# A fused attention, gated-MLP and mixer kernel: half products kept in one accumulator, ScalarE copies between them, sums by accumulating transfers, a new order of all work

## The chip, the core and the metric

The kernel runs on one core of a Trainium2 chip. Its engines each work through their own list of instructions in order: PE (TensorE) multiplies matrices, DVE (VectorE), ACT (ScalarE) and POOL (GpSimd) work element by element, and SP (SyncE) issues most transfers. The metric is device time in microseconds (us); lower is better. Before the change the median of three runs is 398.69 us (397.76 to 398.86).

## The reference: what is computed

Three blocks follow each other, all in float32, on 2 batches of 448 tokens and 768 channels:

```python
# attention, 12 heads of 64
scores = 30 * tanh(q @ k.T / 8 / 30);  attn = exp(scores - max);  x = (attn / sum) @ v
# gated MLP: u, v are the halves of h
h = gelu_tanh(x @ w_in);  v_n = layernorm(v) * g_ln
x = x + (u * (w_sg @ v_n + b_sg)) @ w_out
# mixer: over tokens, then over channels
u = x + (relu(x.T @ w_tok1) @ w_tok2).T
out = u + relu(u @ w_ch1) @ w_ch2
```

## The kernel before, in words

Every product outside attention splits both operands into a high and a low part (fp32r) and multiplies three times, high-high, high-low, low-high. A split is two instructions: `cast` writes the high part on ACT, DVE or POOL, and `rest` subtracts on DVE to get the low part. Weights arrive as 64-bit words; `narrow` turns them into float32 with a scaling of the upper word (line 553 on ACT, 554 on POOL), two ACT passes and DVE passes.

Attention goes over 12 pairs of heads: scores (lines 682, 695), tanh (653) and exp (662) on ACT, values (708, 725), column sums formed on DVE (735, 1290) and summed on PE (757). Its score tiles have two PSUM buffers. While it runs, six rows of `w_in` for v and six for u are narrowed and split, and PE fits in the first products of the gated MLP (line 414).

The last stage, the channel mixer, is two products (`ch1_all`, line 1237 on PE, and `ch2_all`, line 1343) done with seven half-size products each in place of eight (p = 0 to 6) over j = 0 to 5. The sums of operands that this needs are made by DVE additions (`change`, line 1290) or by `gather`, a transfer issued by POOL that adds into its destination (line 1165). The products' sums leave PSUM through `onto`, a DVE addition of a PSUM bank and a tile in SBUF (line 1178). In `ch1_all`, product 0 is copied out by ACT (1266), product 1 is added in the same bank and leaves through a ReLU on ACT (1268), product 2 has a bank of its own, 3 and 4 share one, 5 and 6 share one; five `onto` per j. In `ch2_all` each product runs over all j and three banks before the next.

The order on every engine is set by a planner (`Plan.schedule`). Each operation has a due key, a list of engines that may do it with an estimated duration and a handicap, and the tiles that it reads and writes; the planner simulates the engines and takes the earliest, then the most due. `OFF` shifts keys of single operations, `CH1_ORDER` gives the products' order in `ch1_all`, and `SCALE_ON`, `HI_ON`, `RELU_ON`, `W_ON` say which engines may do what. Tiles come from pools with several buffers (`BUFS`).

Of the kernel before, what the change touches and what calls it, by code (L numbers as in the profile page):

```python
# [32 lines left out]
AHEAD, PACE = (36, 10), 2.2  # L33
# [22 lines left out]
SCALE_ON = {"ch1": {"ACT": 0, "POOL": 200}, "ch2": {"ACT": 0, "POOL": 200}}  # L56
# [30 lines left out]
TURN, STAY = 200.0, 320.8  # L87
TABLE = 1290.0
COLD = 6000.0
EARLY = 74.58  # L90
KQ = 1.69
OFF = {
    "a": {
        (0, 0): 6.9, (0, 1): -3.7, (1, 0): 7.0, (1, 1): 27.0, (1, 2): 12.6, (1, 3): 6.6, (2, 1): 0.7,
        (2, 2): 3.5, (3, 0): 0.7, (3, 2): 8.9, (3, 3): 21.1,
    },
    "d": {
        (8, 0): 1.0,
    },
# [4 lines left out]
    },  # L104
    "f": {
        (0, 0): 1.5, (1, 0): 8.3, (2, 0): 0.4, (3, 0): 1.7, (4, 0): -4.9, (6, 0): -0.7, (7, 0): -0.9,
        (9, 0): -1.6, (10, 0): -7.3, (11, 0): 4.7,
    },
# [4 lines left out]
    },  # L113
# [16 lines left out]
    },  # L130
# [37 lines left out]
class Buf:  # L168


    def __init__(self, tag, shape, dtype):
        self.tag, self.shape, self.dtype = tag, shape, dtype
        self.psum = tag in ("gm", "sc")
        self.ap = None
        self.users = 0
        self.last_writers, self.readers = [], []
        self.end = 0.0
        self.first = None
# [22 lines left out]
class Plan:  # L201
# [40 lines left out]
    def schedule(self):  # L242
# [13 lines left out]
        free = {t: [0.0] * n for t, n in BUFS.items()}  # L256
        for b in {b for o in ops for b in o.bufs if b.tag in free and b.ap is not None}:
            free[b.tag].pop()
# [15 lines left out]
        def earliest(o, way):  # L274
# [7 lines left out]
            for b in o.new:  # L282
                if len(free[b.tag]) <= max(taken[b.tag], queue[b.tag].index(b)):
                    return None
                t = max(t, sorted(free[b.tag])[taken[b.tag]])
                taken[b.tag] += 1
            return t

        while len(order) < len(ops):
# [30 lines left out]
            if o.eng == "PE" and o.mode and t < COLD:  # L320
                dur *= 2
            for w in o.ways:
                ready[w[0]].remove((o, w))
            for b in o.new:
                free[b.tag].sort()
                free[b.tag].pop(0)
# [10 lines left out]
            for b in o.bufs:  # L337
                b.users -= 1
                b.end = max(b.end, o.end + LAT[o.eng])
                if b.users == 0 and b.tag in free:  # L340
                    free[b.tag].append(b.end)
# [9 lines left out]
class Net:  # L351
# [145 lines left out]
    def cast(self, n, out, src, r, w, key=None, on=None, psum=False):  # L497

        nc = self.nc
        made = {  # L500
# [4 lines left out]
                n * 0.84 + 160,  # L505
# [7 lines left out]
    def rest(self, n, out, src, hi, r, w, key=None, on=None, psum=False):  # L513

        nc = self.nc
        args = lambda: dict(out=out(), in0=src(), in1=hi().bitcast(F32), op=ALU.subtract)
# [4 lines left out]
    def split(self, n, hi, lo, src, r, w, key=None, on=None, rest=None, psum=False):  # L521
        self.cast(n, hi, src, r, w, key, on or {"ACT": 0}, psum)
        self.rest(n, lo, src, hi, list(r) + list(w), w, key, rest, psum)
# [1095 lines left out]
```

## Time and profile before

| what | value |
|---|---|
| median of three runs | 398.69 us |
| the profiled execution's own time | 397.94 us |
| its span, first to last instruction | 396.1 us |
| mean granted TensorE clock, share of full speed | 0.997 |
| PE busy | 382.1 us, 96% |
| DVE busy | 328.9 us, 83% |
| ACT busy | 278.9 us, 70% |
| POOL busy | 115.2 us, 29% |

All rows come from one profiled execution, so sums are made against 397.94 us. Of that, 1.84 us lie outside the span. A matmul row's duration includes a pipeline that the next one overlaps, so the pace is read from the distance of starts. Idle time "before" an instruction is followed by what ended it.

### The profile page before, as it was taken

To read this page: it belongs to the slowest core of one execution; us is meant where nothing else is said; L and a number is where in the kernel's file an instruction comes from. 1 tells how busy PE (TensorE), PEld (TensorE's weight loads), DVE (VectorE), ACT (ScalarE), POOL (GpSimd) and SP (SyncE) were. 2 spreads that over 40 slices of the span, in tenths; PEclk is the share of its full clock that TensorE was granted. 3 is DMA by queue.
4 is the path that set the end of the run, shared out by engine and by line. 5 is a ranking of instruction groups with operands and counts; after the bars stand their busy time and mean duration, and the time that the engine had idled before them with its cause. 6 is when DMAs were issued, how large, how long until landed. Compare 5 with 4: busy or idle time off the path is not lost. (4 is left out here: it accounts for less than half of the span.)

```text
span 396.1 us, 6148 instructions
## 1 busy us (share of the span) xinstructions
PE 382.1 (96%) x2048; PEld 293.8 (74%) x2048; DVE 328.9 (83%) x592; ACT 278.9 (70%) x479; POOL 115.2 (29%) x134
## 2 busy tenths in 40 slices
PE   7989999999999999999999999999999999899995
PEld 3222224555578899999999988889999988699984
DVE  1799999988997798947777999997777989987961
ACT  5999999999988678677888787446754472443510
POOL 1001010210022310000043549574431665764200
PEclk9999999999999999999999999999999999999998
DMA  7984445564666638976756998978746795867121
GB/s 241 375 324 126 150 148 171 166 177 129 191 203 205 219 117 273 303 245 181 215 196 166 270 280 175 246 199 199 173 91 173 181 283 113 174 104 123 73 82 68
DMA packets 37772, 74.54 MB, mean 188 GB/s; under 512 B 4449, under 2 KB 25569, under 8 KB 37729
## 3 DMA queue, kind: packets, MB, share of 16 engines
q1 hardware_dynamic: 30240, 63.18, 49.5%
q0 software_dynamic: 7344, 10.75, 16.5%
q8 instruction: 18, 0.29, 0.3%
q14 instruction: 26, 0.20, 0.2%
q10 hardware_dynamic: 144, 0.11, 0.1%
HBM read 50.99 MB, written 12.98 MB: 162 GB/s over the span
## 5 line engine op out<-in xcount | busy, mean ns | idle before, releaser
L1343 PE MATMUL gm<-a,a 128*128 128x448 f32 x252 | 54.9, 366 | 0.0
L1343 PEld LDWEIGHTS gm<-a,a 128*128 128x128 f32 x252 | 47.3, 188 | 3.9
L414 PE MATMUL gm<-a,a 128*128 128x448 f32 (+1 forms) x232 | 46.3, 356 | 0.0
L414 PEld LDWEIGHTS gm<-a,a 128*128 128x128 f32 x232 | 42.0, 188 | 2.1
L662 ACT ACTIVATE a<-a,acap 128x896 f32<-128x896 f32 x42 | 42.7, 1056 | 0.1
L653 ACT ACTIVATE a<-sc,qs 128x896 f32<-128x896 f32 x42 | 41.2, 1017 | 1.3 <-PE sc L682 1.1
L553 ACT ACTIVATE r<-r 128x384 f32<-128x384 f32 (+2 forms) x62 | 36.6, 597 | 3.6 <-DMA r<-ch_in 2.1
L517 DVE TENSOR_TENSOR a<-h,a 128x384 fp32r<-128x384 f32 (+3 forms) x57 | 35.2, 624 | 2.6 <-ACT a L501 1.8
L501 ACT CAST a<-h 128x384 fp32r<-128x384 f32 (+3 forms) x48 | 25.8, 544 | 15.9 <-DMA h<-h 5.7
L1237 PE MATMUL gm<-x,a 128*128 128x448 f32 x162 | 35.9, 369 | 0.6 <-DVE x L517 0.4
L1237 PEld LDWEIGHTS gm<-x,a 128*128 128x128 f32 x162 | 29.9, 188 | 4.7 <-DVE x L517 1.3
L414 PE MATMUL gm<-q,a 128*128 128x448 f32 x160 | 33.2, 366 | 0.0
L1343 PE MATMUL sc<-a,a 128*128 128x448 f32 x126 | 30.5, 371 | 2.1 <-DVE a L517 2.0
L414 PEld LDWEIGHTS gm<-q,a 128*128 128x128 f32 x160 | 30.0, 188 | 2.6
L682 PE MATMUL sc<-q 64*64 64x448 f32 x264 | 30.1, 552 | 1.9 <-ACT a L653 1.7
L708 PE MATMUL gm<-a,v 128*64 128x448 f32 x144 | 31.2, 548 | 0.5 <-ACT a L662 0.2
L414 PE MATMUL gm<-x,a 128*128 128x448 f32 x144 | 30.5, 367 | 0.1
L583 DVE SCALAR_TENSOR_TENSOR t<-r,t 128x384 int32<-128x384 int32 (+2 forms) x40 | 24.3, 610 | 7.4 <-ACT t L575 7.3
L554 POOL TENSOR_SCALAR r<-r 128x384 f32<-128x384 f32 x8 | 11.0, 1380 | 65.9 <-DMA w<-t 60.9
L414 PEld LDWEIGHTS gm<-x,a 128*128 128x128 f32 x144 | 26.8, 188 | 4.4 <-DVE h L788 0.9
L561 ACT ACTIVATE t<-r 128x384 uint16<-128x384 uint16 (+2 forms) x40 | 27.5, 694 | 0.2 <-DVE q L517 0.2
L1343 PEld LDWEIGHTS sc<-a,a 128*128 128x128 f32 x126 | 22.9, 188 | 6.2 <-DVE a L517 4.0
(150 smaller groups left out, 767.2 us busy)
## 6 DMA issues: line engine op xcount, KB each, us to landing
r<-ch_in SPq DMA_DIRECT2D x48, 384.0 KB, 3.8
r<-w_in_in SPq DMA_DIRECT2D x12, 512.0 KB, 5.3
q<-qk_in SPq DMA_DIRECT2D x11, 448.0 KB, 7.0
w<-t SPq DMA_DIRECT2D x24, 192.0 KB, 2.8
v<-va_in SPq DMA_DIRECT2D x12, 256.0 KB, 5.8
r<-w_out_in SPq DMA_DIRECT2D x6, 512.0 KB, 4.9
x<-h SPq DMA_DIRECT2D x12, 224.0 KB, 3.3
h<-x SPq DMA_DIRECT2D x12, 224.0 KB, 4.6
```

The source lines that it names most:

```text
L414: self.nc.tensor.matmul(view(), l, rr, start=(i + m == 0), stop=(i + m == n - 1))
L501: "ACT": ("ACT", n / 1.2 + (60 if psum else 95), lambda: nc.scalar.copy(out(), src()), False),
L517: made = {"DVE": ("DVE", n / 0.96 + 70, lambda: nc.vector.tensor_tensor(**args()), not psum)}
L553: "ACT": ("ACT", n / 1.2 + 130, lambda: nc.scalar.activation(high(), high(), AF.Copy, scale=2.0**-112), False),
L561: lambda: nc.scalar.activation(t.ap.bitcast(U16)[:, 0::2], raw.ap.rearrange("p n t -> p (n t)").bitcast(U16)[:, 1::4], AF.Copy, scale=2.0* ...
L583: lambda: nc.vector.scalar_tensor_tensor(out=t.ap.bitcast(I32), in0=raw[:, :, 1], scalar=3, in1=t.ap.bitcast(I32), op0=ALU.logical_shift_l ...
L653: lambda: nc.scalar.activation(te.ap, sc[:, 0:nn, :S], AF.Tanh, scale=self.qs),
L662: lambda: nc.scalar.activation(te.ap, te.ap, AF.Exp, scale=self.acap),
L682: nc.tensor.matmul(sc[at, h, :S], part(rows, ks), part(rows, QC), start=True, stop=True)
L708: nc.tensor.matmul(A[cols, :S], V[:, 2 * j + h], E[j][:, h], start=(j == 0 and not odd), stop=(j == 2 and odd),)
L1237: nc.tensor.matmul(bank.ap[:, :S], l, r, start=not more and (d, n) == (0, 0), stop=(d, n) == (2, 2), skip_group_check=more)
L1343: nc.tensor.matmul(banks[i].ap[:, :S], l, r, start=not more and (j, n) == (0, 0), stop=(j, n) == (KH - 1, 2), skip_group_check=more,)
```

## The change

Products 0, 2, 5 and 6 (in `ch1_all`) and 0, 2, 4 and 6 (in `ch2_all`) now add up in one accumulator. In `ch1_all` ACT copies the running sum out after each of them (`out_of`); in `ch2_all` ACT does so after 0 and 2 (and after 3, which has the other accumulator), and DVE adds it after 4 and 6. The sign of product 2 is turned in the split of its weights (`sign=-1.0`). The tile c12 is kept negated (`minus_relu`), so that in `ch2_all` the differences of tokens become sums and are made by `gather`. Product 1 in `ch1_all` has a bank of its own. `onto` falls from 45 to 27 instructions, DVE additions of 128x448 (`change`) from 30 to 18, two DVE additions of 128x224 go; ACT copies out of PSUM rise from 9 to 33, ReLUs on ACT of a tile in SBUF from 8 to 14 while the 6 out of a bank go, casts of 128x448 on ACT from 55 to 64. Transfers by `gather` rise from 51 to 63, POOL's casts of weights and tokens (128x384 and 128x448) fall from 40 to 17, its ReLUs from 6 to none. PE's matmuls are the same in number, 756 of them in the two channel products.

Four of the twelve scalings of `w_in` go from ACT to POOL, and POOL's casts of 128x512 rise from one to five. Each tile now has a place in its pool that the planner chose (`slot`); before, only the pool's size was given. The planner's durations for POOL are longer, and all keys in `OFF` are new. The diff, cut:

```diff
-AHEAD, PACE = (36, 10), 2.2
+AHEAD, PACE = (32, 30), 2.2
-SCALE_ON = {"ch1": {"ACT": 0, "POOL": 200}, "ch2": {"ACT": 0, "POOL": 200}}
+SCALE_ON = {"win_v": {"POOL": -200, "ACT": 0}, "win_u": {"POOL": -200, "ACT": 0}, "ch1": {"ACT": 0, "POOL": 200}, "ch2": {"ACT": 0, "POOL": 200}}
+CH1_ORDER += [(2, 0)]
 for j in range(6):
-    CH1_ORDER += [(p, j) for p in ((2, 3, 5, 4, 6) if j < 3 else (0, 2, 3, 1, 5, 4, 6))]
+    CH1_ORDER += [(p, j) for p in (3, 5)] + [(2, j + 1)] * (j < 5) + [(6, j), (4, j)] + [(0, j + 3), (1, j + 3)] * (j < 3)
-    "win_v": ({"DVE": -150}, {"DVE": 0}),
+    "win_v": ({"POOL": -300, "DVE": 0}, {"DVE": 0}),
...
-        (0, 0): 6.9, (0, 1): -3.7, (1, 0): 7.0, (1, 1): 27.0, (1, 2): 12.6, (1, 3): 6.6, (2, 1): 0.7,
+        (0, 0): -1.4, (0, 1): 5.7, (1, 0): 16.8, (1, 1): 29.9, (1, 2): -5.3, (1, 3): 8.0, (2, 0): -0.1,
...
-                    b.ap = pool.tile(b.shape, b.dtype, tag=b.tag, name=f"{b.tag}_{n[b.tag]}", bufs=BUFS[b.tag])
+                    b.ap = pool.tile(b.shape, b.dtype, tag=f"{b.tag}.{b.slot}", name=f"{b.tag}_{n[b.tag]}", bufs=1)
...
+    def out_of(self, out, bank, at):
+        self.act(S, lambda: self.nc.scalar.copy(out.ap, bank.ap[:, :S]), [bank], [out], 60, key=at)
...
             product(0, j, x, a11, o11, False)
-            self.act(S, lambda x=x, o=c12: nc.scalar.copy(o.ap, x.ap[:, :S]), [x], [c12], 60, key=at[0, j])
-            product(1, j, x, a12, o21, True)
-            self.act(S, lambda x=x, o=c11: nc.scalar.activation(o.ap, x.ap[:, :S], AF.Relu), [x], [c11], 60, key=at[1, j])
+            self.out_of(c11, x, at[0, j])
+            product(1, j, w, a12, o21, False)
+            self.onto(c11, w, c11, at[1, j])
+            self.relu(c11, at[1, j])
...
-            product(2, j, y, s2, o2, False)
-            self.onto(c12, y, c12, at[2, j], ALU.subtract)
+            product(2, j, x, s2, o2, True)
+            self.out_of(c21, x, at[2, j])
...
+            product(5, j, x, a21, o1, True)
+            self.out_of(c22, x, at[5, j])
+            self.onto(c22, y, c22, at[5, j])
+            self.relu(c22, at[5, j])
+            product(6, j, x, a12, o22, True)
+            self.out_of(c12, x, at[6, j])
+            self.minus_relu(c12, at[6, j])
+            product(4, j, y, a22, o4, True)
+            self.onto(c21, y, c21, at[4, j])
...
-            self.change(b11[j], b11[j], b12[j], ALU.subtract, S, key(2, j, 16))
-            self.change(t2, b22[j], b11[j], ALU.add, S, key(2, j, 15))
-            product(2, y, j, weight(s2, key(2, j, 9)), tokens(t2, key(2, j, 8)))
+            self.gather(b11[j], b12[j], S, key(2, j, 20) + off("h", 1, j))
+            self.change(t2, b22[j], b11[j], ALU.add, S, key(2, j, 15) + off("h", 2, j))
+            product(2, x, j, weight(s2, key(2, j, 9), -1.0), tokens(t2, key(2, j, 8)), True)
...
-            self.change(b12[j], b22[j], b12[j], ALU.subtract, S, key(3, j, 14))
+            self.gather(b12[j], b22[j], S, key(3, j, 18) + off("h", 3, j))
```

Three places in the lists of instructions follow. The first is ACT at the start of attention: `sc` is a score tile, `a_...<-sc` is tanh, `a<-a,acap` is exp, `r_...` is a raw row of `w_in` being scaled. Before:

```order
L653 ACTIVATE a_189<-sc_165,qs 128x896
L662 ACTIVATE a_189<-a_189,acap 128x896
L553 ACTIVATE r_153<-r_153 128x512
L653 ACTIVATE a_211<-sc_182,qs 128x896
L653 ACTIVATE a_216<-sc_198,qs 128x896
L662 ACTIVATE a_211<-a_211,acap 128x896
L662 ACTIVATE a_216<-a_216,acap 128x896
L653 ACTIVATE a_240<-sc_218,qs 128x896
L653 ACTIVATE a_245<-sc_225,qs 128x896
```

Now:

```order
L680 ACTIVATE a_189<-sc_165,qs 128x896
L689 ACTIVATE a_189<-a_189,acap 128x896
L680 ACTIVATE a_208<-sc_182,qs 128x896
L680 ACTIVATE a_213<-sc_198,qs 128x896
L689 ACTIVATE a_208<-a_208,acap 128x896
L689 ACTIVATE a_213<-a_213,acap 128x896
L680 ACTIVATE a_237<-sc_215,qs 128x896
L680 ACTIVATE a_241<-sc_223,qs 128x896
L689 ACTIVATE a_237<-a_237,acap 128x896
```

The scaling of the raw row between the first exp and the second tanh is gone from ACT, as are two more that came 10 and 13 rows behind it; POOL's first rows behind its memsets are now a scaling, a cast and two more scalings.

The second place is DVE at the head of `ch1_all`: `x_...<-h_...,x_...` is the low part of the operand of product 2, and in the later list `onto` is line 1205, `rest` line 543. Before, the last rows up to it (line 1178 is `onto`, 517 `rest`, 1290 `change`):

```order
L1185 TENSOR_SCALAR h_1730<-h_1730 128x448
L517 TENSOR_TENSOR a_2495<-h_1590,a_2495 128x448
L517 TENSOR_TENSOR a_2519<-v_2210,a_2519 128x384
L517 TENSOR_TENSOR a_2537<-t_2525,a_2537 128x384
L517 TENSOR_TENSOR a_2579<-h_1617,a_2579 128x448
L1290 TENSOR_TENSOR h_1741<-h_1741,h_1590 128x448
L517 TENSOR_TENSOR a_2565<-v_2288,a_2565 128x384
L1290 TENSOR_TENSOR h_1746<-h_1746,h_1610 128x448
L1290 TENSOR_TENSOR h_1806<-h_1806,h_1617 128x448
L517 TENSOR_TENSOR x_2345<-h_1741,x_2345 128x448
```

Now:

```order
L1205 TENSOR_TENSOR q_2518<-q_2518,gm_2534 128x448
L534 SCALAR_TENSOR_TENSOR a_2565<-t_2555,a_2565 128x384
L543 TENSOR_TENSOR a_2371<-v_2182,a_2371 128x384
L1331 TENSOR_TENSOR h_1750<-h_1750,h_1553 128x448
L543 TENSOR_TENSOR a_2572<-a_2276,a_2572 128x384
L543 TENSOR_TENSOR a_2488<-h_1553,a_2488 128x448
L543 TENSOR_TENSOR a_2545<-h_1567,a_2545 128x448
L543 TENSOR_TENSOR a_2510<-h_1557,a_2510 128x448
L1205 TENSOR_TENSOR q_2539<-q_2539,gm_2579 128x448
L610 SCALAR_TENSOR_TENSOR h_2601<-r_2467,h_2601 128x384
L1331 TENSOR_TENSOR h_1785<-h_1785,h_1557 128x448
L543 TENSOR_TENSOR x_2344<-h_1750,x_2344 128x448
```

Counted from the last addition of the token mixer (line 1137 before, 1164 now), the low part of the first operand of product 2 is the 23rd row before and the 22nd now. On PE, product 2 follows the six products (0, j) and (1, j) of j = 0 to 2 at once now; before, product (5, 0) stood between them.

The third place is POOL in `ch2_all`, about where product 1 runs. `TENSOR_SCALAR` is a cast, `DMA` a gather; `x`, `q` and the `a` of a `q<-a` are tokens, all others weights. Before:

```order
L506 TENSOR_SCALAR a_3466<-h_3050 128x384
L1165 DMA v_2707<-a_3392 128x384
L1165 DMA v_2788<-a_3426 128x384
L506 TENSOR_SCALAR a_3511<-x_3206 128x448
L506 TENSOR_SCALAR a_3537<-x_3214 128x448
L1165 DMA a_3392<-a_3392 128x384
L1165 DMA h_2888<-t_3544 128x384
L1165 DMA a_3426<-a_3426 128x384
L1165 DMA v_2824<-a_3501 128x384
L1165 DMA h_3002<-t_3565 128x384
L506 TENSOR_SCALAR a_3616<-v_2601 128x384
L506 TENSOR_SCALAR a_3624<-v_2668 128x384
```

Now:

```order
L1192 DMA v_2587<-h_2846 128x384
L1192 DMA q_2518<-q_2518 128x448
L1192 DMA v_2700<-h_2967 128x384
L1192 DMA q_2539<-q_2539 128x448
L1192 DMA v_2734<-h_3039 128x384
L1192 DMA q_2720<-q_2720 128x448
L1192 DMA q_2584<-q_2584 128x448
L1192 DMA q_2920<-q_2920 128x448
L1192 DMA q_2518<-a_2672 128x448
L1192 DMA v_2741<-h_3129 128x384
L1192 DMA v_2814<-h_3182 128x384
L1192 DMA v_3020<-h_3219 128x384
```

The casts have left the list, and transfers that add tokens to tokens (`q<-q`, `q<-a`) have come in.

## Rows read from the trace of the kernel before

**Rows 1.** Windows: stretch, length, busy (xinstructions) of PE, PEld, DVE, ACT, POOL; clock, DMA.
```profile
0.00:62.00 62.00, 55.32 (x390) 17.23 (x392) 49.49 (x81) 56.36 (x65) 3.94 (x12) 1.00 0.67 231
110.00:232.00 122.00, 122.00 (x625) 110.21 (x624) 99.48 (x183) 95.62 (x185) 23.76 (x29) 1.00 0.71 220
232.00:256.00 24.00, 23.26 (x111) 20.18 (x110) 23.52 (x48) 16.28 (x35) 18.23 (x16) 1.00 0.95 222
312.00:348.00 36.00, 33.89 (x162) 29.46 (x162) 34.28 (x64) 15.87 (x32) 23.73 (x23) 1.00 0.84 189
```

**Rows 2.** PE's list in attention: start, duration, instruction, [idle before <-releaser].
```profile
10.29 0.59 PE L695 MATMUL sc<-a,a 64*64 64x448 f32 x2 [1.77 <-ACT a L653]
...
16.98 0.97 PE L757 MATMUL gm<-a,ones 128*64 128x448 f32 x4 [0.23 <-DVE a L1290]
...
26.04 1.51 PE L682 MATMUL sc<-q 64*64 64x448 f32 x12 [1.75 <-ACT a L653]
...
40.45 0.97 PE L757 MATMUL gm<-a,ones 128*64 128x448 f32 x4 [0.48 <-DVE a L1290]
```

**Rows 3.** ACT's list at the start of attention.
```profile
8.68 0.65 ACT L553 ACTIVATE r<-r 128x512 f32<-128x512 f32 x1 [1.20 <-DMA r<-w_in_in]
9.24 1.89 ACT L653 ACTIVATE a<-sc,qs 128x896 f32<-128x896 f32 x2
...
17.42 0.68 ACT L553 ACTIVATE r<-r 128x512 f32<-128x512 f32 x1
```

**Rows 4.** DVE's list, at the start and at the head of ch1_all.
```profile
9.83 1.42 DVE L605 SCALAR_TENSOR_TENSOR t<-r,t 128x512 int32<-128x512 int32 x2
...
12.35 1.15 DVE L735 SCALAR_TENSOR_TENSOR a<-a,guard,a 128x896 f32<-128x896 f32 x1
...
233.67 0.61 DVE L1137 TENSOR_TENSOR h<-gm,h 128x448 f32<-128x448 f32 x1
...
245.17 0.62 DVE L517 TENSOR_TENSOR x<-h,x 128x448 fp32r<-128x448 f32 x1
```

**Rows 5.** POOL's lines (ns min/median/max): scaling, casts, gathers; how long transfers land.
```profile
L554 POOL TENSOR_SCALAR r<-r x8: 1232/1290/1675, 200.9 to 280.8; 128x384 f32<-128x384 f32 x8
L506 POOL TENSOR_SCALAR a<-v x11: 502/531/5355, 208.8 to 344.9; 128x384 fp32r<-128x384 f32 x11
L1165 POOL DMA_DIRECT2D h<-h x10: 869/917/2647, 245.2 to 294.3; - x10
DMA to landing us min/median/max: 3.0/4.7/12.1
```

**Rows 6.** PE's list at the head of ch1_all, and a piece without a wait.
```profile
245.07 0.36 PE L1237 MATMUL gm<-x,a 128*128 128x448 f32 x1
245.85 4.10 PE L1237 MATMUL gm<-x,a 128*128 128x448 f32 x17 [0.41 <-DVE x L517]
249.79 1.99 PE L1237 MATMUL gm<-a,a 128*128 128x448 f32 x9
...
312.47 1.99 PE L1237 MATMUL gm<-x,a 128*128 128x448 f32 x9
314.30 2.60 PE L1343 MATMUL gm<-a,a 128*128 128x448 f32 x12
```

**Rows 7.** PE's list in ch2_all.
```profile
337.86 0.97 PE L1343 MATMUL sc<-a,a 128*128 128x448 f32 x4
339.42 0.67 PE L1343 MATMUL sc<-a,a 128*128 128x448 f32 x2 [0.60 <-DVE a L517]
...
344.19 1.33 PE L1343 MATMUL sc<-a,a 128*128 128x448 f32 x4
346.43 0.67 PE L1343 MATMUL sc<-a,a 128*128 128x448 f32 x2 [0.92 <-DVE a L517]
```

**Rows 8.** DVE's list in ch2_all, an addition behind a ReLU of POOL.
```profile
325.15 0.62 DVE L1290 TENSOR_TENSOR q<-q 128x448 f32<-128x448 f32 x1 [1.22 <-POOL q L1194]
```

**Rows 9.** Groups by line: busy us, mean ns of one, idle before.
```profile
L1266 ACT COPY q<-gm 128x448 f32<-128x448 f32 x6 | 3.2, 528 | 1.0 <-PE gm L1237 1.0
```

More of the change, by code (lines that the diff above doesn't have):

```diff
@@ L255, in schedule @@
             queue[tag] = [e[2] for e in q]
-        free = {t: [0.0] * n for t, n in BUFS.items()}
+        free = {t: [(0.0, i) for i in range(n)] for t, n in BUFS.items()}
         for b in {b for o in ops for b in o.bufs if b.tag in free and b.ap is not None}:
-            free[b.tag].pop()
+            free[b.tag].remove((0.0, b.slot))
         ready = defaultdict(list)
@@ L321, in schedule @@
                 dur *= 2
+            if o.eng == "DVE":
+                dur += 18.0
             for w in o.ways:
@@ L495, in consts, with cast @@
         self.plan.op([("PE", 800 + 480 * WARM, spin, False, 0)], -30.0, [], [warm])
-    def cast(self, n, out, src, r, w, key=None, on=None, psum=False):
+    def cast(self, n, out, src, r, w, key=None, on=None, psum=False, sign=1.0):
         nc = self.nc
+        if sign < 0:
+            turn = lambda e: e.tensor_scalar(out(), src(), -1.0, None, ALU.mult)
+            made = {
+                "ACT": ("ACT", n / 1.2 + 95, lambda: nc.scalar.activation(out(), src(), AF.Copy, scale=-1.0), False),
+                "DVE": ("DVE", n / 1.92 + 70, lambda: turn(nc.vector), True),
+                "POOL": ("POOL", n * 2.5 + 190, lambda: turn(nc.gpsimd), False),
+            }
+            ways = [made[e] + (t,) for e, t in on.items()]
+            return self.plan.op(ways, self.key - 8 if key is None else key, r, w)
         made = {
@@ L511, in cast, with rest @@
         return self.plan.op(ways, self.key - 8 if key is None else key, r, w)
-    def rest(self, n, out, src, hi, r, w, key=None, on=None, psum=False):
+    def rest(self, n, out, src, hi, r, w, key=None, on=None, psum=False, sign=1.0):
         nc = self.nc
+        if sign < 0:
+            return self.dve(
+                n,
+                lambda: nc.vector.scalar_tensor_tensor(
+                    out=out(), in0=src(), scalar=-1.0, in1=hi().bitcast(F32), op0=ALU.mult, op1=ALU.subtract
+                ),
+                r,
+                w,
+                key=key,
+                port=True,
+            )
         args = lambda: dict(out=out(), in0=src(), in1=hi().bitcast(F32), op=ALU.subtract)
@@ L519, in rest, with split @@
         return self.plan.op(ways, self.key - 8 if key is None else key, r, w)
-    def split(self, n, hi, lo, src, r, w, key=None, on=None, rest=None, psum=False):
-        self.cast(n, hi, src, r, w, key, on or {"ACT": 0}, psum)
-        self.rest(n, lo, src, hi, list(r) + list(w), w, key, rest, psum)
+    def split(self, n, hi, lo, src, r, w, key=None, on=None, rest=None, psum=False, sign=1.0):
+        self.cast(n, hi, src, r, w, key, on or {"ACT": 0}, psum, sign)
+        self.rest(n, lo, src, hi, list(r) + list(w), w, key, rest, psum, sign)
     def weight(self, src, n, key, name, after=None):
@@ L1164, in gather @@
         self.plan.op(
-            [("POOL", 1000.0, lambda: nc.gpsimd.dma_start(out=out.ap, in_=a.ap, accum_op=ALU.add), False, 0)],
+            [("POOL", 1150.0, lambda: nc.gpsimd.dma_start(out=out.ap, in_=a.ap, accum_op=ALU.add), False, 0)],
             at,
@@ L1303, in ch2_all @@
         whole = [self.buf("x", [128, 4, S]) for _ in range(KH)]
-        pairs = [self.a([128, 2, 384]) for _ in range(KH)]
+        pairs = [self.a([128, 2, 384]) for _ in range(KH // 2)]
         rows = lambda i: [Part(x, lambda ap: ap[:, i]) for x in whole]
@@ L1307, in ch2_all @@
         a12 = [self.h([128, 384]) for _ in range(KH)]
[L1308 removed]
+        a21 = [self.h([128, 384]) for _ in range(KH)]
+        a22 = [Part(pairs[j // 2], lambda ap, j=j: ap[:, j % 2]) for j in range(KH)]
         part, spare = rows(0), rows(3)
@@ L1373, in ch2_all @@
         for i in three:
-            t = part[i]
-            self.act(S, lambda i=i, t=t: nc.scalar.copy(t.ap, x[i].ap[:, :S]), [x[i]], [t], 60, key=key(1, 0, 4))
+            self.out_of(part[i], x[i], key(1, 0, 4))
+            self.gather(U[0][i], part[i], S, key(1, 0))
         for j in js:
-            product(1, x, j, weight(a12[j], key(1, j, 9)), tokens(b21[j], key(1, j, 8)), True)
+            product(1, w, j, weight(a12[j], key(1, j, 9)), tokens(b21[j], key(1, j, 8)))
         for i in three:
-            z = U[0][i]
-            self.onto(z, x[i], z, key(2, 0))
-            store(z, i, 0, key(2, 1))
-        y = banks()
+            u = U[0][i]
+            self.onto(u, w[i], u, key(2, 0))
+            store(u, i, 0, key(2, 1))
         for j in js:
@@ L1394, in ch2_all @@
+            self.gather(b12[j], b22[j], S, key(3, j, 18) + off("h", 3, j))
+            self.gather(a21[j], a22[j], 384, key(4, j, 20))
         for i in three:
-            self.onto(part[i], y[i], part[i], key(3, 0), ALU.subtract)
-        z = banks()
+            self.out_of(part[3 + i], x[i], key(3, 0, 4))
+            self.gather(U[0][3 + i], part[3 + i], S, key(3, 0))
+        y = banks()
         for j in js:
-            product(3, z, j, weight(a11[j], key(3, j, 9)), tokens(b12[j], key(3, j, 8)))
+            product(3, y, j, weight(a11[j], key(3, j, 9)), tokens(b12[j], key(3, j, 8)))
@@ L1399, in ch2_all @@
         for i in three:
-            self.onto(part[3 + i], z[i], part[i], key(4, 0, 4))
-            u = U[0][3 + i]
-            self.gather(u, part[i], S, key(4, 0))
+            self.out_of(part[i], y[i], key(4, 0, 4))
+            self.gather(U[1][3 + i], part[i], S, key(4, 0))
         for j in js:
-            product(4, z, j, weight(a22[j], key(4, j, 9)), tokens(b21[j], key(4, j, 8)), True)
+            product(4, x, j, weight(a21[j], key(4, j, 9)), tokens(b11[j], key(4, j, 8)), True)
+        for i in three:
+            u = U[1][3 + i]
+            self.onto(u, x[i], u, key(5, 0, 4))
+            store(u, 3 + i, 1, key(5, 1))
@@ L1405, in ch2_all @@
+        for j in js:
+            product(5, y, j, weight(a22[j], key(5, j, 9)), tokens(b21[j], key(5, j, 8)), True)
         for i in three:
             u = U[0][3 + i]
-            self.onto(u, z[i], u, key(5, 0))
-            store(u, 3 + i, 0, key(5, 1))
-            u = U[1][3 + i]
-            self.gather(u, part[3 + i], S, key(5, 0))
-            u = U[1][i]
-            if i < 2:
-                self.gather(u, part[i], S, key(5, 1))
-                continue
-            for n, o in enumerate(self.last_out):
-                cs = slice(n * S // 2, (n + 1) * S // 2)
-                self.combine(
-                    S // 2,
-                    lambda o=o: o.ap,
-                    lambda u=u, cs=cs: u[:, cs],
-                    lambda i=i, cs=cs: part[i].ap[:, cs],
-                    ALU.add,
-                    [u, part[i]],
-                    [o],
-                    key(5, 3),
-                )
@@ L1427, in ch2_all @@
-        v = banks(self.last_bank)
-        for j in js:
-            product(5, v, j, weight(a21[j], key(5, j, 9)), tokens(b11[j], key(5, j, 8)))
-        for i in three:
-            u = U[1][3 + i]
-            last = self.onto(u, v[i], u, key(6, 0, 4))
-            store(u, 3 + i, 1, key(6, 0))
+            last = self.onto(u, y[i], u, key(6, 0, 4))
+            store(u, 3 + i, 0, key(6, 0))
         if not self.anycap:
@@ L1437, in ch2_all @@
         for j in js:
-            product(6, v, j, weight(a12[j], key(6, j, 9)), tokens(b22[j], key(6, j, 8)), True)
+            product(6, x, j, weight(a12[j], key(6, j, 9)), tokens(b22[j], key(6, j, 8)), True)
         for i in range(2):
             u = U[1][i]
-            self.onto(u, v[i], u, key(6, 5))
+            self.onto(u, x[i], u, key(6, 5))
             store(u, i, 1, key(6, 5))
```

114 lines of the change are left out of this document (59 added, 55 removed), and 53 rows, old and new, of the table OFF.

## The prediction

> **What bounds the kernel now.** I read the windows first, then the waits of PE, then the lists of the engines that PE waited for. In the windows the reader is to see that PE is the bound nearly everywhere: from 110 to 232 us it is busy in 122.00 of 122.00 us [rows 1]. The change leaves PE's matmuls as they are in number, so a gain can come only out of the time in which PE stands. That time is small and lies in three places: attention (55.32 us busy of the first 62), the head of `ch1_all` (23.26 of 24) and a stretch of `ch2_all` (33.89 of 36). In the last two DVE is as full as PE, 23.52 of 24 and 34.28 of 36; in attention it is ACT that is full, 56.36 of 62 with its start-up in it.
>
> PE's list in attention shows whom it waited for: 1.77 us at 10.29 and 1.75 us at 26.04 for a tanh on ACT, which has to free one of two score tiles, and 0.23 and 0.48 us for DVE's sums [rows 2]. ACT's list tells why: between its first exp and its second tanh it stood 1.20 us until a raw row of `w_in` had landed and then scaled it, 9.24 - 8.68 = 0.56 us; together 1.76 us, PE's first wait. Two more such scalings follow within 3 us, the first at 17.42 [rows 3].
>
> In the channel mixer I measure PE's loss by its pace: nine matmuls without a wait take 314.30 - 312.47 = 1.83 us, 0.203 each. At the head of `ch1_all` one matmul takes 245.85 - 245.07 = 0.78 us, a loss of 0.58, and the next 17 take 3.94 us, a loss of 0.48; 1.06 together [rows 6]. In `ch2_all` four matmuls take 1.56 and 2.24 us where 0.81 would do: 0.75 and 1.43 lost [rows 7], and a third such place before them I take at 0.7, about the smaller of the two; 2.9 us together.
>
> **The change, part by part.** *Attention.* Four of twelve scalings and a few casts leave ACT and DVE for POOL, which is busy 3.94 us of the first 62 [rows 1]. At the start ACT goes from its first exp straight to the next tanh: 1.76 us earlier. Not all of it stays. The first row's conversion on DVE now waits for POOL, and DVE does its work in order, so the first column sums stand behind it. POOL's scaling of 384 elements takes at least 1.23 us [rows 5], so 512 take an estimated 1.64: ready at 8.68 + 1.64 = 10.3 in place of 9.24. Behind it DVE has three conversions (two took 1.42, a third an estimated 0.4), three additions of about 1.15 each and one low part (about 0.6) [rows 4]: 10.3 + 1.8 + 3.5 + 0.6 = 16.2. PE's first sum was at 16.98 [rows 2] and can now be at about 16.3: 0.7 us gained there. ACT keeps the rest as a lead over PE, and without the two further scalings it should not be waited for at 26.04; I count that 1.75 us as gone. Of the waits for DVE's sums I count nothing. Term: -2.5 us. Bounds: -4.2 (the four waits of rows 2 all gone) and +1.5 (POOL late, below).
>
> *110 to 232 us.* PE has no idle time there, so the new order can only add; DVE's 99.48 of 122 us leaves room. I take +0.3, bounds 0 and +1.5.
>
> *Head of `ch1_all`.* PE first needs the six products (0, j) and (1, j), 54 x 0.203 = 11.0 us, and then product 2. Before, product 5 stood between, nine matmuls or 1.83 us of cover. DVE's way to the first operand of product 2 is hardly shorter: 22 rows behind the token mixer's last addition where it was 23, and these took 245.17 - 233.67 = 11.5 us [rows 4], so 0.5 each. Two `onto` of product 1, which DVE did not have to do before, are among them. DVE gets there 0.5 us sooner and PE 1.83 us sooner: the first wait grows from 0.58 to about 1.9, and most of the second (0.48) goes, as PE comes later. Term: 1.9 - 1.06 = +0.8 us. Bounds: -1.06 (no wait) and +2.5.
>
> *Rest of `ch1_all`.* Two `onto` fewer per j on DVE, two copies more on ACT of 0.528 us [rows 9]. The copy stands on PE's path: product 6 may add to the accumulator only when product 5 has been copied out. One product stands between, 1.83 us; copy and an ACT instruction in progress (0.65, rows 3) take 1.18. Hidden, so 0; if ACT is one more instruction behind, it costs nothing still, two more 0.65 for each of six j, +3.9.
>
> *`ch2_all`.* Twelve additions of tokens and six `onto` leave DVE, at about 0.6 us (the like row: 0.61) [rows 4], plus two halves: some 11 us of the 34.28 busy in 36 [rows 1] and what follows. POOL loses its ReLUs and nearly all casts there; DVE stood 1.22 us behind one such ReLU [rows 8]. ACT takes six more copies, 3.2 us, beside 15.87 us busy in 36. DVE is then ahead of PE by several us where it was behind, and I count 2.5 of the 2.9 us as gone. Bounds: -2.9 and +4 (the transfers, below). The new transfers replace additions that DVE did itself. From the last use of the tokens to the addition that needs their sum there are 20 rows on DVE, 10 us at 0.5; issue and landing take 0.92 + 4.7 us in the median [rows 5]. Hidden, so 0.
>
> Tile places: they decide which earlier reader a write waits for; the trace does not price them apart, and they are in the bounds.
>
> Sum: -2.5 + 0.3 + 0.8 - 2.5 = -3.9 us, on 397.94 us: 394.0. The median of the runs is 0.75 above the profiled execution; I add half of it: 394.4 us.
>
> At one place a rule speaks against this. POOL's cast of 384 elements took 0.53 us in the median and 5.36 at most [rows 5]. The Trainium skill (SBUF — State Buffer, Who interferes with whom) says that a DVE instruction with two SBUF inputs contends with a GpSimd instruction that reads SBUF. The trace agrees in that the factor of ten is there. By that rule the nine scalings and casts that now run on POOL in attention, beside DVE's additions, would be long ones, and attention's term would be nearer its bound of +1.5 than -2.5; I hold to -2.5, because in the first 20 us DVE waits for POOL rather than working beside it. What the rule would make of the whole is the second rival.
>
> **The rivals.** *The head of `ch1_all` grows (396.8 us).* PE's wait for product 2 becomes 3.5 us, its bound of +2.5, and copies by ACT cost another 0.7: for it, DVE is full there (23.52 of 24); against it, DVE has a row less. 394.4 + (2.5 - 0.8) + 0.7 = 396.8.
>
> *POOL's work in attention takes its gain back (398.2 us, no change).* Each of the nine operations has DVE work behind it. If three of them are as long as 5.36 us and DVE stands 1.22 us behind each, as in rows 8, that is 3.7 us: 394.4 + 3.7 = 398.1. For it: the longest cast; against it: POOL is idle 58 of 62 us, so most are done early.
>
> *Transfers of tokens land late (401 us, slower).* In `ch2_all` DVE's addition for product 2 waits for its gather and everything behind waits too. It decides from a landing of 10 - 0.9 = 9.1 us on. Landing reached 12.1 and an issue on POOL 2.65 [rows 5]: 3.0 + 1.7 = 4.7 us late. One such wait, and one of 3 us behind it, is 7.7 us, less 1 us of lead that I leave to DVE: 394.4 + 6.7 = 401.1. For it: twelve more transfers on one queue; against it: the median of 4.7.
>
> **How the numbers follow.** Forecast 0.60, with its own range of 391.5 to 396.5; head of `ch1_all` 0.15; no change 0.14; slower 0.11. A measurement of this kernel tells 0.3% from no change, 397.5 to 399.9 us around 398.69. The first two cases are faster, 0.75 and a little of the third, 0.01; same 0.13; slower 0.11. The range of 8 in 10 goes from 391.0, a little inside the sum of the good bounds (398.3 - 4.2 - 1.06 - 2.9 = 390.1), to 398.2, which takes in the no-change case and leaves out the late transfers.
>
> **What would show it.** Right: no ACT scaling between the first exp and the second tanh, PE's fifth group of matmuls at about 8.5 us in place of 10.29, no wait above 0.5 us for a tanh after 20 us; one wait of 1 to 2.5 us for `x` on DVE at the first product 2; no PE wait for DVE in `ch2_all`, where DVE should show idle time, and POOL nothing but gathers. Wrong: PE waiting for ACT's copy in `ch1_all` at each j; DVE waiting for DMA in front of the additions of `ch2_all`; a PE wait anywhere between 110 and 232 us; a DVE wait for POOL's casts in attention of more than a microsecond.

## The result, and the profile after

The changed kernel takes 393.61 us (median of four runs, 393.18 to 394.10) against 398.31 of the kernel before: a ratio of 0.9882, 95% interval 0.986 to 0.9905. The forecast was 394.4. The profiled execution took 394.1 us with a span of 391.9, the slowest of the four.

The total came out, but not by the forecast's terms: attention fell 2.2 us short of its term and the channel mixer went 2.4 us past its own. That the two cancel is luck. I set three marks on TensorE's list in both traces: the first 128x128 matmul behind the last sums of attention, the first matmul of `ch1_all`, and the modelled end of the last one of `ch2_all`.

| stretch | before, us | after, us | difference | forecast |
|---|---|---|---|---|
| start to end of attention | 115.44 | 115.12 | -0.3 | -2.5 |
| on to the head of `ch1_all` | 116.53 | 116.73 | +0.2 | +0.3 |
| channel mixer, 756 matmuls | 159.84 | 155.74 | -4.1 | -1.7 |
| rest of the profiled execution's own time | 6.13 | 6.51 | +0.4 | 0 |

The windows that answer to [rows 1], in the same columns:

```profile
0.00:62.00 62.00, 56.49 (x400) 18.35 (x400) 50.00 (x82) 56.56 (x63) 16.09 (x20) 1.00 0.67 232
110.00:232.00 122.00, 121.77 (x621) 109.65 (x620) 99.48 (x184) 99.83 (x197) 12.69 (x18) 1.00 0.68 211
232.00:256.00 24.00, 22.37 (x109) 19.75 (x108) 23.82 (x46) 18.64 (x39) 12.91 (x16) 1.00 1.11 266
312.00:348.00 36.00, 36.00 (x180) 33.39 (x179) 33.41 (x66) 18.67 (x40) 25.40 (x30) 1.00 1.14 197
```

The last row shows the gain: TensorE has no idle time from 312 to 348 us, 180 matmuls where there were 162. In `ch2_all` its list names no wait at all, where [rows 7] had 0.60 and 0.92 us.

In attention it is otherwise. TensorE's list, answering to [rows 2]:

```profile
8.67 0.97 PE L722 MATMUL sc<-a,a 64*64 64x448 f32 x4
10.80 0.59 PE L722 MATMUL sc<-q 64*64 64x448 f32 x2 [1.16 <-DMA q<-qk_in]
...
17.64 0.97 PE L784 MATMUL gm<-a,ones 128*64 128x448 f32 x4 [1.05 <-DVE a L1331]
...
24.72 1.88 PE L709 MATMUL sc<-q 64*64 64x448 f32 x16 [0.38 <-ACT a L680]
...
43.07 0.97 PE L784 MATMUL gm<-a,ones 128*64 128x448 f32 x4 [0.49 <-DVE a L1331]
```

The two waits of 1.77 and 1.75 us for a tanh are gone: the fifth group starts at 8.67 instead of 10.29, and at 24.72 only 0.38 us is left. But directly behind the fifth group TensorE now waits 1.16 us for the second pair's keys, and at the first sums 1.05 us for VectorE. GpSimd's list, then VectorE's, say why the sums are late:

```profile
9.46 1.57 POOL L581 TENSOR_SCALAR r<-r 128x512 f32<-128x512 f32 x1 [7.55 <-DMA r<-w_in_in]
13.02 1.46 POOL L521 TENSOR_SCALAR a<-t 128x512 fp32r<-128x512 f32 x1 [2.00 <-DVE t L632]
14.63 2.24 POOL L581 TENSOR_SCALAR r<-r 128x512 f32<-128x512 f32 x1
```

```profile
11.06 0.43 DVE L621 TENSOR_SCALAR t<-r 128x512 int32<-128x512 int32 x1 [6.04 <-POOL r L581]
11.52 1.42 DVE L632 SCALAR_TENSOR_TENSOR t<-r,t 128x512 int32<-128x512 int32 x2
12.86 1.15 DVE L762 SCALAR_TENSOR_TENSOR a<-a,guard,a 128x896 f32<-128x896 f32 x1
14.11 1.31 DVE L1331 TENSOR_TENSOR a<-a,a 128x896 f32<-128x896 f32 x1
15.34 1.15 DVE L543 TENSOR_TENSOR a<-t,a 128x512 fp32r<-128x512 f32 x1
16.42 1.07 DVE L1331 TENSOR_TENSOR a<-a,a 64x896 f32<-64x896 f32 x1
```

VectorE stands until GpSimd has scaled the raw row at 11.03, then does three conversions of `w_in`, and only then the three additions that the first sums wait for (L762 and twice L1331).

At the head of `ch1_all` there is one wait of the size forecast, at another tile. TensorE's list, answering to [rows 6]:

```profile
242.67 6.95 PE L1277 MATMUL gm<-x,a 128*128 128x448 f32 x33 [1.51 <-DVE q L1205]
```

It stands not at product 2 for operand `x` but one product sooner, at product 1 of the third j, which needs the accumulator that VectorE's addition (242.00 to 242.61) has yet to read.

### The profile page after: what moved, and what is told of

Read it like the earlier page. It is cut to its first block, busy times and chain, and to the rows that moved or that the text cites. A ratio compares the mean times of both kernels' runs of the same rounds, so it can differ in the third digit from the quotient of the medians.

```text
span 391.9 us, 6112 instructions
## 1 busy us (share of the span) xinstructions
PE 380.2 (97%) x2048; PEld 295.6 (75%) x2048; DVE 312.9 (80%) x571; ACT 298.1 (76%) x523; POOL 94.5 (24%) x116
## 5 line engine op out<-in xcount | busy, mean ns | idle before, releaser
L543 DVE TENSOR_TENSOR a<-h,a 128x384 fp32r<-128x384 f32 (+3 forms) x63 | 36.8, 587 | 5.5 <-ACT a L516 4.9
L516 ACT CAST a<-h 128x384 fp32r<-128x384 f32 (+3 forms) x56 | 29.9, 537 | 14.3 <-DVE h L1071 4.8
L580 ACT ACTIVATE r<-r 128x384 f32<-128x384 f32 (+2 forms) x66 | 38.4, 584 | 2.0 <-DMA r<-ch_in 1.7
L709 PE MATMUL sc<-q 64*64 64x448 f32 x264 | 31.0, 552 | 1.0 <-ACT a L680 0.9
L735 PE MATMUL gm<-a,v 128*64 128x448 f32 x144 | 30.4, 548 | 0.1
L1390 PE MATMUL sc<-a,a 128*128 128x448 f32 x126 | 28.7, 364 | 0.0
L602 ACT ACTIVATE t<-r 128x384 f16<-128x384 f32 (+2 forms) x40 | 27.8, 694 | 0.0
L1331 DVE TENSOR_TENSOR a<-a,a 128x896 f32<-128x896 f32 (+1 forms) x24 | 26.6, 1108 | 0.4
```

Source lines behind the costliest of these rows:

```text
L516: "ACT": ("ACT", n / 1.2 + (60 if psum else 95), lambda: nc.scalar.copy(out(), src()), False),
L543: made = {"DVE": ("DVE", n / 0.96 + 70, lambda: nc.vector.tensor_tensor(**args()), not psum)}
L580: "ACT": ("ACT", n / 1.2 + 130, lambda: nc.scalar.activation(high(), high(), AF.Copy, scale=2.0**-112), False),
L602: lambda: nc.scalar.activation(t.ap.bitcast(F16)[:, 1::2], raw[:, :, 1].bitcast(F32), AF.Copy, scale=sign),
L709: nc.tensor.matmul(sc[at, h, :S], part(rows, ks), part(rows, QC), start=True, stop=True)
L735: nc.tensor.matmul(A[cols, :S], V[:, 2 * j + h], E[j][:, h], start=(j == 0 and not odd), stop=(j == 2 and odd),)
```

## The experiments

Two theories of the channel mixer's 4 us: A, VectorE was the bound there and was relieved; B, tiles' planned places took waits for earlier readers away. For attention: ScalarE's freed time was gained and lost again at VectorE and at a transfer; or it never bound. All medians are against 398.28 to 398.78 of the kernel before on the same chips.

**1 and 2. Tile places.** The changed kernel with pools in rotation, and the kernel before with planned places; every engine's order stays.

```
- tag=f"{b.tag}.{b.slot}", ..., bufs=1
+ tag=b.tag, ..., bufs=BUFS[b.tag]
```

> The changed kernel with one thing undone: a tile takes the next place of its pool in turn, as before the change, and not the place that the planner freed. No engine's order changes. Theory A (the 3.9 us that the channel mixer gained come from relief of VectorE: additions into transfers, sums copied out by ScalarE): 393.2 to 394.6 us, no wait of TensorE beyond those of the changed kernel. Theory B (planned places took waits for a tile's last reader away, and that is the gain): 396 to 398.5 us, with waits of TensorE or VectorE in the second channel product that the changed kernel doesn't have.

> The kernel before with one part of the change: tiles get the place that the planner freed. No engine's order changes. Theory A (relief of VectorE is the gain): 397.3 to 398.7 us, with the three waits of TensorE for VectorE in the second channel product (331, 339 and 346 us; 2.0 us together) still there. Theory B (places are the gain): 394.5 to 396.5 us and those waits gone or below 0.8 us together.

Measured: 394.45 us (0.9897, 0.9879 to 0.9915) and 398.29 us (0.999, 0.9969 to 1.0011). Planned places alone give nothing. The list of waits of TensorE in that run (engine, tile, line; total, times, longest) has the three waits of `ch2_all` in full, in its second row:

```profile
PE sc L683 <- ACT a L654: 2.1, 2, 1.7
PE sc L1344 <- DVE a L518: 2.0, 3, 0.9
PE sc L696 <- ACT a L654: 1.6, 1, 1.6
```

With the planned places undone in the changed kernel the median is 0.8 us higher, which the two intervals don't separate; its trace has one wait more, at the head of `ch1_all`, for a copy by ScalarE:

```profile
253.28 0.87 PE L1277 MATMUL gm<-a,a 128*128 128x448 f32 x3 [1.26 <-ACT a L1228]
```

Theory B fails as the source of the gain.

**3. Twelve token additions back on VectorE.**

The two `gather` calls for b11 and b12 (cut) become, at the same places of the order:

```
+ nc.vector.tensor_tensor(out=out.ap, in0=out.ap, in1=a.ap, op=ALU.add)
```

> The changed kernel with the twelve additions of token tiles in the second channel product (b11 and b12, 128x448) on VectorE instead of in transfers, at the same places in the order. VectorE gets 12 x 0.535 us = 6.4 us more; it is 33.41 of 36.00 us busy from 312 to 348 us. Theory A: the slack of 2.6 us there is used up, waits of TensorE for VectorE come back, 395 to 397.5 us. Theory B (places): 393.2 to 394.3 us, no such wait. A third possibility, that VectorE's additions are ready earlier than a transfer (0.6 us against some 5 us), so that nothing is lost: 393 to 394 us.

Measured: 396.17 us (0.9941, 0.992 to 0.9963), 2.6 above the changed kernel, as theory A says. TensorE's list in `ch2_all`, then windows of that run:

```profile
338.17 0.36 PE L1401 MATMUL sc<-a,a 128*128 128x448 f32 x1
340.07 0.68 PE L1401 MATMUL sc<-a,a 128*128 128x448 f32 x2 [1.54 <-DVE a L543]
341.17 1.09 PE L1401 MATMUL sc<-a,a 128*128 128x448 f32 x3 [0.43 <-ACT a L509]
342.08 2.43 PE L1401 MATMUL gm<-a,a 128*128 128x448 f32 x6
344.31 1.93 PE L1401 MATMUL sc<-a,a 128*128 128x448 f32 x6
346.08 3.80 PE L1401 MATMUL gm<-a,a 128*128 128x448 f32 x18
```

```profile
337.00:340.00 3.00, 1.53 (x8) 1.09 (x6) 3.00 (x7) 0.00 (x0) 0.00 (x0) 1.00 0.66 201
340.00:342.00 2.00, 1.50 (x5) 0.83 (x6) 2.00 (x6) 0.98 (x2) 1.22 (x2) 1.00 0.25 94
342.00:344.00 2.00, 2.00 (x7) 1.77 (x7) 1.80 (x5) 0.93 (x2) 1.52 (x3) 0.52 0.93 149
344.00:346.00 2.00, 2.00 (x8) 1.79 (x7) 1.97 (x5) 0.93 (x2) 1.35 (x2) 0.63 0.96 151
346.00:348.00 2.00, 2.00 (x12) 1.85 (x11) 0.79 (x2) 0.46 (x1) 0.28 (x1) 1.00 1.02 167
```

VectorE is busy without a gap from 337 to 342 us while TensorE waits for it. The clock column of these windows belongs to the last section; the profiled execution is the slowest of six (398.13 us), and with 397.83 one of two that stand apart: the other four took 395.63 to 396.44. So the additions cost these four 2.0 to 2.8 us against the changed kernel's median.

**4. The four scalings back on ScalarE.** `nc.gpsimd.tensor_scalar(high(), ...)` becomes `nc.scalar.activation(high(), ..., scale=2.0**-112)`, places unchanged.

> The changed kernel with the four w_in scalings (128x512) that it has on GpSimd during attention issued by ScalarE at the same places of the order. Theory A (the freed ScalarE time was worth some 2 us, and the changed kernel lost it again at the wait for the second pair's keys, 1.16 us, at the first sums, 1.05 us, and by more changes of TensorE's tile shapes, 0.6 us): giving the time back to ScalarE costs 1 to 3 us, 394.6 to 396.6 us; the end of attention moves from 115.12 to 116 or later. Rival (ScalarE's time doesn't bind in attention, the matmuls do): 393.2 to 394.2 us and the end at 115.1 to 115.5.

Measured: 395.16 us (0.9917, 0.9899 to 0.9934), 1.5 above the changed kernel; attention ends at 116.43 us. Both long waits for a tanh are back in TensorE's list:

```profile
10.20 0.59 PE L722 MATMUL sc<-a,a 64*64 64x448 f32 x2 [1.89 <-ACT a L680]
...
25.94 1.50 PE L709 MATMUL sc<-q 64*64 64x448 f32 x12 [1.91 <-ACT a L680]
```

So these scalings caused the two waits, and in this order their removal is worth 1.5 us, not the 3.8 us that the waits measure.

**5 and 6. What took the rest: the sums' place, or the keys?** VectorE's list is changed by setting the start by which an operation is sorted:

```
+ MOVED = {334: 13300.0, 335: 13400.0, 336: 13500.0, 337: 13600.0, 338: 14200.0}   # w_in behind the sums' additions
+ (second run) 332: 2110.0                                     # the first w_in load behind the second pair's keys
```

> The changed kernel with VectorE's first three w_in operations (tile t, behind GpSimd's scaling at 9.46 us) moved behind the second addition of the first pair's sums, and its fourth behind the third addition; nothing else moves. In the changed kernel the sums' additions stand behind them and TensorE waits 1.05 us at 17.64 us. Theory A (that order is what took the gain of attention): first sums at 16.4 to 16.9 us, and 0.6 to 1.1 us of it is still there at the end of attention (115.12 us before): 392.5 to 393.2 us. Rival (ScalarE, busy almost throughout from 11 us, sets the pace whatever the sums do): sums earlier, but the end of attention at 114.9 to 115.3 and 393.3 to 394.0 us.

> As the run with the sums' additions first, and in addition the load of the second pair's keys and queries is issued ahead of the first w_in load (512 KB) instead of behind it. Theory A: the wait of 1.16 us at 10.80 us goes, TensorE's fifth group starts at 9.6 to 10.0 us, ScalarE follows a whole us earlier, the end of attention at 113.0 to 113.8 and 391.3 to 392.3 us. Rival (what comes early is given back, since w_in's rows come later or ScalarE paces): 392.8 to 394 us.

Measured: 392.66 us (0.9851, 0.9822 to 0.9881) and 392.54 us (0.9847, 0.9817 to 0.9878). The sums' order gives 0.95 us, the theory's figure. VectorE's list of the first run:

```profile
10.57 1.15 DVE L769 SCALAR_TENSOR_TENSOR a<-a,guard,a 128x896 f32<-128x896 f32 x1 [5.46 <-ACT a L696]
11.83 1.09 DVE L1338 TENSOR_TENSOR a<-a,a 128x896 f32<-128x896 f32 x1
12.84 0.43 DVE L628 TENSOR_SCALAR t<-r 128x512 int32<-128x512 int32 x1
13.30 1.45 DVE L639 SCALAR_TENSOR_TENSOR t<-r,t 128x512 int32<-128x512 int32 x2
14.67 1.08 DVE L1338 TENSOR_TENSOR a<-a,a 64x896 f32<-64x896 f32 x1
```

Two additions are done before the conversions start, TensorE's first sums come at 15.89 in place of 17.64, and attention ends at 113.83. The other profiles with the sums first and the loads in their old order (runs 11 and 12) end it at 113.77 and 114.54, where six without it had 114.8 in the mean. The load's order adds nothing that the medians show: in the second run the keys land at 7.39 us in place of 9.69 and the raw row of `w_in` at 9.22 in place of 8.32, and the median moves by 0.12 us, less than theory A asked for. The first of the two runs has no wait for keys either, with SP's order unchanged. Executions with the same order up to there waited 0 to 1.27 us for these keys (last section), so the 1.16 us of the profile above is no fixed price.

**7 and 8. The head of `ch1_all`.**

In words, both runs give product (1, 2) its accumulator in place "sc.1", idle until 249 us. The second run also puts VectorE's four rows for `x` and their two additions ahead of `onto(1, 1)`, and ScalarE's copy of `x` (its cast to the high part) ahead of a ReLU.

> The changed kernel with one accumulator moved: product 1 of the third j (its sixth product) gets a bank of a pair that stands idle until 249 us, and so doesn't wait at 242.67 us (1.51 us) for VectorE's addition at 242.00. No order changes. Theory A (behind that wait stands the one forecast, for the low part of operand x at 243.54 to 244.15 us): TensorE waits some 1.2 us one product later, gain 0.2 to 0.5 us, 393.1 to 393.5 us. Rival (the bank was the only wait): gain 1.2 to 1.5 us, 392.1 to 392.4 us.

> As the run with the accumulator moved, and VectorE makes the parts of operand x (tiles x, h) ahead of the addition at 242.00 us and of the merge of raw weights behind it; ScalarE's ReLU of the sum moves behind its copy of x. Theory A: both waits at the head go but for some 0.5 us, gain 0.8 to 1.4 us against the changed kernel, 392.2 to 392.8 us. Rival (given back at the next products, 251.88 and 253.50 us, since VectorE has no idle time up to 256 us): 393.2 to 394.0 us.

Measured: 393.31 us (0.9867, 0.9837 to 0.9897) and 394.33 us (0.9894, 0.9863 to 0.9925). With its own bank product (1, 2) starts at once, and TensorE waits for the operand that the forecast named:

```profile
240.67 1.98 PE L1280 MATMUL aside<-x,a 128*128 128x448 f32 x9
242.49 0.37 PE L1280 MATMUL gm<-x,a 128*128 128x448 f32 x1
243.66 5.09 PE L1280 MATMUL gm<-x,a 128*128 128x448 f32 x23 [0.81 <-DVE x L546]
```

By pace (a stretch's length less 0.2033 us for each matmul in it) the head up to 265 us loses 2.1 us, against 2.3 in the changed kernel and 2.1 in runs 3, 5 and 10 with the old bank: the wait only moved. The second run is slower than both of its theories. In it ScalarE stood 2.63 us at the copy of `x` that I had moved forward, until VectorE had made `h`; all that ScalarE had behind it came later, and TensorE then waited for ScalarE three times (0.75, 0.17, 0.63 us):

```profile
244.05 0.57 ACT L526 CAST x<-h 128x448 fp32r<-128x448 f32 x1 [2.63 <-DVE h L1343]
```

**9. The kernel before, with its first four scalings on GpSimd and nothing else moved.**

> The kernel before with one part of the change: the first four w_in scalings (128x512) are issued by GpSimd at the places where ScalarE had them; nothing else moves. The forecast's term for attention was -2.5 us for taking them off ScalarE: by it the end of attention comes at 113.0 us and the run at 395.6 to 396.2. Theory A (the relief is worth the 1.5 us that the run with the scalings back on ScalarE showed, and VectorE's additions for the sums then stand behind GpSimd's scaling, which takes 1.6 us and more against 0.65): end of attention at 114 to 115 us, TensorE's first sums with a wait of 0.5 to 1.5 us, 396.6 to 397.6 us. Rival (the order of the changed kernel is needed for any gain): 398.0 to 398.6 us.

Measured: 399.74 us (1.0018, 0.9999 to 1.0036) against 398.78: no gain, where the forecast's term by itself would have given 2.5 us. Attention ends at 116.58. GpSimd's and VectorE's rows around the last of the four:

```profile
23.87 1.15 DVE L741 SCALAR_TENSOR_TENSOR a<-a,guard,a 128x896 f32<-128x896 f32 x1
24.12 4.61 POOL L558 TENSOR_SCALAR r<-r 128x512 f32<-128x512 f32 x1 [6.81 <-DVE t L600]
24.93 0.69 DVE L611 SCALAR_TENSOR_TENSOR t<-r,t 128x512 int32<-128x512 int32 x1
25.53 1.09 DVE L1296 TENSOR_TENSOR a<-a,a 128x896 f32<-128x896 f32 x1
26.53 0.70 DVE L611 SCALAR_TENSOR_TENSOR t<-r,t 128x512 int32<-128x512 int32 x1
27.27 1.45 DVE L1296 TENSOR_TENSOR a<-a,a 64x896 f32<-64x896 f32 x1
```

The same operation took 1.58 us at 8.59, while VectorE stood. TensorE's waits for VectorE's sums grow to 1.80 us at 17.49 and 1.11 at 39.91. The first wait for a tanh is gone; the second is still 1.32 us, at 25.83. My expectation (396.6 to 397.6) was too good; nearest is the rival, that the relief needs the new order, and the median lies 1.1 us above its range too. The profiled execution is the fastest of twelve (397.65 us), so these rows show where attention's gain went, not what made the median 1 us worse.

**10. Six copies of `ch2_all` on VectorE.** `nc.scalar.copy` becomes `nc.vector.tensor_copy` behind products 2 and 3.

> The changed kernel with the six copies out of accumulators behind products 2 and 3 of the second channel product on VectorE instead of ScalarE, at the same places of the order. VectorE gets 6 x 0.535 = 3.2 us more. Theory A (the token additions in transfers carry the gain of the second channel product; at the places of the copies VectorE has room, 25.08 of 39.59 us busy from 348 us, and the banks are not wanted at once): 393.2 to 394.2 us, no wait of TensorE. Rival (the copies on ScalarE are as needed as the transfers): 394.6 to 396 us with waits of TensorE for VectorE in the second channel product.

Measured: 394.02 us (0.9883, 0.986 to 0.9906); the channel mixer takes 155.54 us, with no wait in `ch2_all`. These copies carry nothing of the gain.

**11 and 12. Gains together.** The sums first and the bank; then also VectorE's rows for `x` early, with ScalarE's order left alone.

> The changed kernel with the sums' additions ahead of the first w_in operations on VectorE and the sixth product's own accumulator, both as in their runs. If the two gains (0.95 and 0.3 us) add: 392.1 to 392.6 us, faster than either kernel; if the wait for operand x takes the second back: 392.5 to 393.0 us.

> As the run with the sums first and the sixth product's own accumulator, and on VectorE the parts of operand x come directly behind the addition of product 1 of the second j, with the two merges of raw weights behind them; ScalarE's order stays as it is (in the run that moved its copy of x too, ScalarE stood 2.63 us). Theory A: TensorE's wait of 0.81 us for x falls to some 0.5 us or less, nothing waits for ScalarE that didn't before, 391.6 to 392.3 us. Rival (VectorE has no idle time here, so the merges come later and the wait only moves to the next weights): 392.3 to 393.3 us.

Measured: 392.67 us (0.9844, 0.9818 to 0.9869) and 393.71 us (0.9871, 0.9848 to 0.9895). The bank adds nothing to the sums' 392.66. With `x` early its wait falls from 0.81 to 0.34 us, but TensorE then waits 0.82 us for a copy by ScalarE and the head loses 3.0 us by pace; the run is slower than both of its theories. VectorE is full there (23.82 us of the 24 from 232 in the changed kernel); in both runs that put the rows for `x` first, something else came late. The best versions are those with the sums first (392.5 to 392.7 us); no run of the first of them (392.04 to 393.0) is as slow as the fastest of the changed kernel (393.18).

## Why the prediction was right in its total and wrong in two terms

*Attention, -2.5: mis-sized.* The mechanism held: the scalings made the waits for a tanh, and these went (run 4). The step that failed is "ACT keeps the rest as a lead over PE", with "now be at about 16.3" for the first sum. The scaling began at 9.46, when its row had landed, instead of 8.68 (the other five profiles with this order have that landing at 8.20 to 9.18, so this is an execution's bad luck in part); VectorE's rows beside GpSimd's were longer than I took (1.31 for 1.15, 1.15 for 0.6); the sum came at 17.64. Run 5 prices VectorE's order at 0.95 us. That the new order by itself makes TensorE's work longer, 0.6 us for changes of tile shape as I expected before run 4, is not shown: up to the end of attention, waits over 0.15 us taken off, TensorE takes 109.6 us where it took 109.0, but seven profiles with the new order have 108.9 to 110.1, and their first product with the values starts anywhere from 7.19 to 7.95 us. Six profiles with the changed kernel's order there (this one, runs 1, 3, 7, 8 and 10) end attention at 114.4 to 115.3 us, 114.8 in the mean, so the term is nearer -0.7 than this execution's -0.3. The new order alone (run 4), the relief alone (run 9) and both end attention at 116.4, 116.6 and 114.8 us, where the kernel before gave 115.4, and 115.7 with other tile places (run 2): neither part helps by itself, as far as one profile of each can tell. What exactly costs 1 us in the new order with the scalings on ScalarE was not taken apart.

*110 to 232 us, +0.3:* +0.2 by the marks.

*Head of `ch1_all`, +0.8:* +0.3. By pace the channel mixer up to 265 us lost 2.05 us before and 2.32 after; runs 3, 5 and 10, with the changed kernel's order there, lost 2.1, so the head hardly changed. The first wait has the forecast's size (1.5 to 1.7 for 1.9) but another cause: I overlooked that the first three products 1 take turns in one accumulator. The forecast's own cause stands right behind it (run 7), which is why removing the bank's wait bought nothing.

*Rest of `ch1_all`, 0:* ScalarE's copies are hidden as forecast; no wait per j. By pace 265 to 325 us got 0.6 better; I had not counted these small losses.

*`ch2_all`, -2.5:* -3.8, past the good bound of -2.9. The mechanism is right: run 3 gives back 2.6 us with the twelve additions alone, run 10 nothing with the copies. Too small was the stock of loss: from 325 us on it is 3.5 us by pace in the kernel before, where I counted 2.9, and after the change the matmuls take in sum 0.3 us less than 0.2033 each, so that nothing is left over. The stock varies: in run 9, which has the kernel before's order there, the same stretch lost 1.9 us, its waits at 331 and 339 us all but gone, so -3.8 is the price of this pair of executions. What makes up the remaining microsecond or so beside the additions (GpSimd's ReLUs and casts, or the order) was not tried.

*Tile places:* nothing alone, 0.8 us at most in the new order. *Half of the difference to the median, +0.4:* the profiled execution is this time the slowest, and the median lies 0.5 below it.

*Rivals.* The head grew by less than its price. Transfers of tokens landed late by the forecast's measure: those of `q` tiles took 7.2 and 8.8 us in the median where I used 4.7, close to the 9.1 from which that rival decides, and three of the twelve took 9.4 to 11.8. The profile's DMA issues (tile, queue, count, size, median us to landing), and VectorE's only wait for a transfer in `ch2_all`, for an output tile:

```profile
q<-q POOLq DMA_DIRECT2D x6, 224.0 KB, 7.2
q<-a POOLq DMA_DIRECT2D x6, 224.0 KB, 8.8
```

```profile
DVE x L1205 <- DMA x<-x: 0.6, 1, 0.6
```

No addition of tokens waited, so the lead was longer than the rival took. GpSimd's work taking back the gain of attention is no mere rival: run 9 is that case. The scaling that took 4.61 us beside VectorE's additions, and 1.58 alone, is the row for it. The Trainium skill (SBUF — State Buffer, Who interferes with whom) says that a VectorE instruction with two SBUF inputs contends with a GpSimd instruction that reads SBUF; the trace agrees with these two durations, though no run sets the contention apart. In the changed kernel the four scalings took 1.57 to 2.45 us. Two bounds of the prediction don't match what they point to (+1.5 against 3.7 - 2.5 = 1.2, and +4 against the late transfers' 6.7); its forecast doesn't rest on them.

## What to carry to other kernels

Taking work off a full engine is worth the whole wait that it caused only if nothing that stands in order on the receiving side comes later: here 3.8 us of waits were worth 1.5, and nothing in the old order. Move the urgent additions ahead of the work that waits for the slower engine; that one reorder gave another 0.95 us. Price a stretch by its matmuls' pace, not by named waits alone, and before you remove a wait, look for a second one right behind it. Before a small difference at the start of a kernel is explained, see how much the landing of its first loads varies between executions.

## What the hardware showed that I had not expected

- In run 3 TensorE did only two matmuls between 338.53 and 341.17 us, and three more up to 342.08; then the granted clock fell to 0.52 and 0.63 for 342 to 346 us, which is mostly the lower of its two levels, and was back at 1.00 from 346. The twelve matmuls from 342.08 to 346.08 took 4.00 us in place of 2.44: 1.6 us on top of the waits. That execution took 398.13 us, five others 395.63 to 397.83. The kernel before, whose three waits there are shorter and further apart, shows 1.00 throughout them.
- The load of the second pair's keys, issued at 3.05 us with the same order before it, landed at 9.37, 9.46, 10.35, 10.46, 10.76 and 10.29 us in six executions alike up to there (runs 8, 10, 1 with other tile places, 7, the changed kernel, run 3). TensorE waited for it not at all twice, and 0.58, 0.70, 1.16 and 1.27 us: more than many of the effects studied here.
